# Turning keys and queries in 64-row tiles, both in one block, each row half into its own PSUM bank

## The chip, the core and the metric

The kernel runs on one core of a Trainium2 chip. Times are device microseconds of one launch; the kernel before took 110.33 us (the median of three runs, 109.01 to 110.8). The engines of the core are named as the profile names them: PE (TensorE; PEld is its loading of weights), DVE (VectorE), ACT (ScalarE), POOL (GpSimd) and SP (SyncE, which here issues the loads and stores). The profile shows one execution.

## What is computed

Two layers follow each other: a linear attention with decay, in blocks of 64 positions, and a highway layer over the 512 features that it gives. The inputs are q, k and v of 4 batches x 8 heads x 768 positions x 64, and two 512 x 512 weight matrices.

```
for b in range(nb):                       # 12 blocks of 64 positions
    qb, kb, vb = q[:, :, sl], k[:, :, sl], v[:, :, sl]
    intra = einsum('bhic,bhjc->bhij', qb, kb) * Dmask
    intra = einsum('bhij,bhjd->bhid', intra, vb)
    inter = einsum('bhid,bhde->bhie', qb * lam_pow, kv_state)
    out[:, :, sl] = intra + inter
    kv_state = lam_block * kv_state + einsum('bhsd,bhse->bhde', kb * rev_pow, vb)
x = out.transpose(0, 2, 1, 3).reshape(3072, 512)
H = maximum(x @ w_h, 0);  T = sigmoid(x @ w_t + b_t)
result = T * H + (1 - T) * x
```

## The kernel before

The kernel works in 12 steps of 256 positions (three to a batch), each in two blocks of 128. What runs, in which order, is written out in a string, PLAN: each word is a token, such as `TQ.2.2=5` or `EK.2.2@DVE`. The part before the first dot is the operation, the first number is the step, `@` names the engine that does it, and `=` lists the PSUM banks that it takes, of seven that go around (0 to 6; the eighth holds the running state kv). A table DO gives the function for each token. Every engine executes its own tokens in the order of the plan; waits between engines are put in from the data, the buffers and the banks. A block that takes a bank waits until the last reader of the bank's former content is done. The tokens that matter here, for a step n:

- Lk, Lq, Lv: loads on SP's queue (L192, L195). CK, CQ, CV: the casts to bf16, with the decay for q and v, into kb, qb and vs (from the third step on mostly on POOL, L104, L217, L212).
- TK, TQ: eight full 128 x 128 transposes of keys (L236) or queries (L231) on PE into one bank each. EK, EQ: one copy of 1024 columns out of that bank, into kT or qT (on ACT at L102 or on DVE at L104).
- SS.n.e: scores of n (L253), paired with updates of the state (L258), in 64 x 64 tiles. It needs all of kT and qT. M: the causal mask on DVE (L292), four to a step. KE: a copy of the state (ss).
- I: the part of the output that comes from the state (L308, needs qT and ss). A: the part within a block (L318, needs M). D: copies of the result to xT (L102, L104).
- F.n.u.w: eight matmuls of the highway layer (L336; w is 0 for H, bank bh, and 1 for T, bank bt), u one half of the features. H: relu and difference on DVE (L341). G: two sigmoids on ACT (L350), in place in the bank. X: the product on DVE (L354), which reads that bank last.
- R: turning back, 32 matmuls of 64-row tiles, the row halves alternating between two banks (L383). E: copies of these to o (L102, L104). ST: the store.
- Z: matmuls on zeros at the start (L402).

SS, A, U and S work in 64 x 64 tiles of the array, R of a whole step in 64 x 128 tiles, all others on the full array. kT and qT have two buffers each, kb three and qb two.

Of the kernel before, what the change touches and what calls it, by code (L numbers as in the profile page):

```python
# [14 lines left out]


PLAN = """
Lk.0.0 Lv.0.1 Lv.0.0 Lq.0.0 Lk.0.1 Lq.0.1 Lv.1.1 CK.0.0@POOL Lq.1.0 Z.12=0 TK.0.0=0 Lq.1.1 CV.0.0@DVE Lk.1.0
CQ.0.0@POOL EK.0.0@DVE Lv.1.0 CV.0.1@DVE CK.0.1@ACT Lk.1.1 Z.11=1 TQ.0.0=1 B=2 EQ.0.0@ACT CQ.0.1@POOL W.0.1 W.0.0
Z.6=0 TQ.0.1=3 TK.0.1=4 EQ.0.1@DVE U.0.0 EK.0.1@ACT W.1.1 S.0.0=56 KE.0.0@DVE S.0.1=01 CQ.1.2@POOL W.1.0 M.0.0.1 Z.1=3  # L20
U.0.1 I.0=34 M.0.1.1 KE.0.1@ACT Lk.2.1 M.0.0.0 A.0.1 M.0.1.0 TQ.1.2=0 Lq.2.1 CV.1.2@DVE CK.1.2@ACT EQ.1.2@ACT Lq.2.0
Z.8=1 TK.1.2=1 A.0.0 EK.1.2@DVE Lk.2.0 D.0.0@DVE Z.3=5 SS.1.1=56 WC.0.0.1@ACT WC.0.0.0@POOL M.1.1.0 KE.1.0@ACT
WC.0.1.0@POOL D.0.1@ACT Lv.2.1 WC.0.1.1@DVE Z.4=0 SS.1.0=01 M.1.1.1 I.1=35 KE.1.1@ACT Lv.2.0 F.0.0.0=4 WC.1.1.0@DVE PT
M.1.0.1 Lk.3.1 F.0.1.0=6 M.1.0.0 WC.1.0.0@POOL WC.1.0.1@ACT Lk.3.0 WC.1.1.1@DVE A.1.1 A.1.0 BC F.0.0.1=1 H.0.1 Lq.3.1
D.1.1@ACT H.0.0 D.1.0@ACT F.0.1.1=0 Lq.3.0 CQ.2.2@POOL F.1.0.0=2 Lv.3.0 G.0.1@ACT CK.2.2@DVE F.1.0.1=6 Lv.3.1
G.0.0@ACT X.0.1@DVE TQ.2.2=5 Lq.4.0 X.0.0@DVE TK.2.2=4 EQ.2.2@ACT CV.2.2@POOL F.1.1.0=3 Lq.4.1 EK.2.2@DVE G.1.0@ACT
H.1.0 SS.2.0=01 Lk.4.1 H.1.1 CK.3.2@POOL SS.2.1=54 Lk.4.0 M.2.0.1 F.1.1.1=2 KE.2.0@ACT M.2.1.0 Lv.4.0 TK.3.2=3 M.2.1.1
CQ.3.2@POOL G.1.1@ACT I.2=15 M.2.0.0 Lv.4.1 A.2.1 X.1.0@DVE A.2.0 Lk.5.0 R.0=40 D.2.0@ACT D.2.1@DVE CV.3.2@POOL
TQ.3.2=6 E.0.0@ACT Lk.5.1 F.2.1.1=1 E.0.1@ACT EQ.3.2@DVE Lq.5.1 EK.3.2@ACT X.1.1@DVE F.2.1.0=5 CQ.4.2@POOL Lq.5.0
R.1=40 H.2.1 SS.3.1=62 Lv.5.0 F.2.0.0=3 CK.4.2@POOL KE.3.0@ACT M.3.1.1 Lv.5.1 E.1.1@ACT M.3.1.0 SS.3.0=52 E.1.0@ACT  # L30
H.2.0 Lq.6.0 TQ.4.2=0 KE.3.1@ACT CV.4.2@POOL M.3.0.1 TK.4.2=6 G.2.1@ACT Lq.6.1 F.2.0.1=4 M.3.0.0 EQ.4.2@ACT EK.4.2@DVE
Lv.6.0 I.3=32 A.3.0 CK.5.2@POOL A.3.1 Lk.6.1 SS.4.1=56 D.3.0@ACT D.3.1@DVE TK.5.2=0 KE.4.0@ACT M.4.1.1 Lk.6.0
F.3.0.0=2 G.2.0@ACT CQ.5.2@POOL EK.5.2@DVE Lv.6.1 SS.4.0=36 H.3.0 F.3.0.1=0 Lq.8.0 M.4.0.0 CV.5.2@POOL M.4.0.1
TQ.5.2=2 Lk.9.0 G.3.0@ACT F.3.1.0=3 X.2.1@DVE Lq.7.0 EQ.5.2@ACT X.2.0@DVE F.3.1.1=6 CQ.6.2@POOL M.4.1.0 Lq.7.1
KE.4.1@ACT I.4=14 H.3.1 G.3.1@ACT R.2=25 Lk.8.1 X.3.0@DVE A.4.0 E.2.1@ACT X.3.1@DVE A.4.1 Lk.7.1 SS.5.0=30 E.2.0@ACT
D.4.0@DVE CK.6.2@POOL SS.5.1=56 D.4.1@ACT Lk.7.0 TQ.6.2=2 M.5.0.0 KE.5.0@ACT CV.6.2@POOL TK.6.2=1 M.5.1.1 Lv.7.0
EQ.6.2@ACT F.4.1.0=4 M.5.0.1 Lv.7.1 EK.6.2@ACT F.4.0.0=3 H.4.1 Lk.8.0 M.5.1.0 I.5=62 SS.6.1=01 H.4.0 Lq.8.1 A.5.0
KE.6.0@ACT M.6.1.0 CQ.7.2@POOL R.3=45 Lv.9.1 A.5.1 M.6.1.1 SS.6.0=30 D.5.0@ACT Lv.8.0 F.4.0.1=1 M.6.0.0 D.5.1@ACT
M.6.0.1 Lk.9.1 TQ.7.2=6 G.4.0@ACT CK.7.2@POOL F.5.0.0=3 Lq.10.1 EQ.7.2@ACT F.4.1.1=2 H.5.0 Lk.10.1 E.3.1@ACT X.4.0@DVE
TK.7.2=0 CV.7.2@POOL G.4.1@ACT I.6=63 ST.0 KE.6.1@DVE F.5.0.1=5 X.4.1@DVE Lv.8.1 F.5.1.0=1 G.5.0@ACT CK.8.2@POOL  # L40
EK.7.2@DVE Lq.9.0 A.6.0 E.3.0@ACT H.5.1 A.6.1 SS.7.1=20 Lq.9.1 D.6.0@ACT D.6.1@DVE TK.8.2=4 M.7.1.1 F.6.1.0=1 Lv.9.0
EK.8.2@ACT X.5.0@DVE CK.9.2@POOL F.6.1.1=6 KE.7.0@DVE Lk.10.0 CQ.8.2@POOL H.6.1 R.4=30 SS.7.0=54 Lk.11.1 E.4.0@ACT
F.5.1.1=1 E.4.1@ACT M.7.0.1 G.6.1@ACT ST.4 M.7.1.0 TK.9.2=3 Lq.10.0 M.7.0.0 TQ.8.2=0 G.5.1@ACT CV.8.2@POOL F.6.0.0=4
EQ.8.2@DVE Lk.11.0 KE.7.1@ACT X.5.1@DVE I.7=25 EK.9.2@ACT Lq.11.0 A.7.0 H.6.0 A.7.1 CQ.9.2@POOL SS.8.0=01 X.6.1@DVE
D.7.1@ACT Lv.10.1 SS.8.1=34 M.8.0.1 D.7.0@ACT F.6.0.1=6 KE.8.0@DVE Lq.11.1 CK.10.2@POOL F.7.0.0=5 M.8.1.0 G.6.0@ACT
M.8.1.1 ST.3 TQ.9.2=1 CV.9.2@POOL H.7.0 F.7.1.0=2 EQ.9.2@ACT Lv.10.0 X.6.0@DVE TK.10.2=3 M.8.0.0 ST.1 I.8=45
EK.10.2@ACT CQ.10.2@POOL H.7.1 SS.9.1=61 A.8.1 KE.9.0@ACT M.9.1.0 A.8.0 R.5=02 M.9.1.1 SS.9.0=36 CK.11.2@POOL
E.5.1@DVE F.7.0.1=1 KE.9.1@ACT M.9.0.1 E.5.0@ACT F.7.1.1=2 D.8.0@DVE D.8.1@ACT ST.5 CQ.11.2@POOL M.9.0.0 G.7.0@ACT
Lv.11.1 TK.11.2=6 Lv.11.0 I.9=04 F.8.1.0=5 EK.11.2@ACT ST.2 X.7.0@DVE TQ.10.2=3 G.7.1@ACT H.8.1 CV.10.2@POOL F.8.0.0=1
EQ.10.2@ACT R.6=65 H.8.0 A.9.1 X.7.1@DVE A.9.0 SS.10.1=31 D.9.0@ACT D.9.1@DVE F.8.1.1=2 E.6.1@ACT M.10.1.1 F.9.1.0=0  # L50
E.6.0@DVE G.8.1@ACT M.10.1.0 ST.6 TQ.11.2=4 CV.11.2@POOL KE.10.0@DVE F.9.1.1=5 EQ.11.2@ACT X.8.1@DVE SS.10.0=16
G.9.1@ACT H.9.1 R.7=32 M.10.0.1 KE.10.1@ACT F.8.0.1=4 X.9.1@DVE E.7.0@ACT M.10.0.0 E.7.1@ACT I.10=06 SS.11.0=53
G.8.0@ACT ST.7 A.10.0 M.11.0.0 A.10.1 SS.11.1=21 D.10.1@ACT X.8.0@DVE F.9.0.0=5 KE.11.0@ACT M.11.1.0 D.10.0@ACT
F.9.0.1=6 M.11.0.1 M.11.1.1 F.10.1.0=4 G.9.0@ACT H.9.0 I.11=20 X.9.0@DVE A.11.0 A.11.1 R.8=31 D.11.0@ACT R.9=56
E.8.0@ACT F.10.0.0=2 E.9.0@DVE E.9.1@ACT E.8.1@ACT D.11.1@DVE ST.9 F.10.1.1=3 H.10.0 ST.8 F.10.0.1=6 H.10.1 G.10.1@ACT
F.12.1.1=5 G.10.0@ACT X.10.1@DVE F.11.1.1=1 F.11.1.0=0 G.12.1@ACT X.10.0@DVE F.11.0.1=2 G.11.1@ACT H.11.1 F.12.1.0=4
R.10=36 G.11.0@ACT H.12.1 X.11.1@DVE F.11.0.0=0 E.10.0@ACT X.12.1@DVE F.12.0.1=4 E.10.1@ACT H.11.0 F.12.0.0=1
G.12.0@ACT X.11.0@DVE ST.10 R.11.1.1=5 H.12.0 R.11.0.2=3 E.11.1.1@DVE X.12.0@DVE E.11.0.2@ACT ST.11.1.1 R.11.1.0=0
ST.11.0.2 E.11.1.0@DVE ST.11.1.0
"""  # L60

BUFS = dict(kf=5, qf=5, vf=5, kb=3, qb=2, vs=3, kT=2, qT=2, m=8, xT4=2, th4=2, xT2=3, xT1=2, th2=2, th1=2, hm2=3, hm1=2, tb2=2, tb1=2, ss=4, o=5, oh=2, oq=1)
# [3 lines left out]
def kernel(  # L66
# [13 lines left out]
    C = 128  # L80
# [4 lines left out]
    J = 2  # L85
# [11 lines left out]
    def half(e):  # L97
        return slice(64 * e, 64 * e + 64)
# [80 lines left out]
    def get(*key):  # L179
        return made[key]  # L180
# [57 lines left out]
    def evac_k(n, p, eng):  # L238
        hs = heads(p)
        copy(eng, new(("kT", n), [128, NP, J, C])[:, hs.start // 2:hs.stop // 2], get("ktr", n, p))  # L240

    def evac_q(n, p, eng):
        hs = heads(p)
        if n:
            copy(eng, new(("qT", n), [128, NP, 2 * C]).rearrange("e h (p j) -> e h p j", j=Q),
                 get("qtr", n, p).rearrange("e j (p h) -> e h p j", h=NP))
            return
        copy(eng, new(("qT", n), [128, NP, 2 * C])[:, hs.start // 2:hs.stop // 2].rearrange("p n (c j) -> p n c j", j=J),
             get("qtr", n, p).rearrange("p n j c -> p n c j"))


    def score(n, e, hp, j, b):
        T.matmul(get("s", n, e, hp // 2)[half(b), hp % 2, j, :], lhsT=get("kT", n)[half(e), hp, j, half(b)],  # L253
                 rhs=get("qT", n)[half(e), hp, b * C:(b + 1) * C], start=True, stop=True)
# [6 lines left out]
    def scores_state(n, e, bk):  # L261
        for u in range(2):
            bank(("s", n, e, u), bk[u], [128, 2, J, C])
        b = 1 - e
        st = [(hp, j, x) for hp in range(NP) for j in range(J) for x in range(2)]
        if b == 1 and n % NST == NST - 1:
            st = []
        for i, (hp, j, x) in enumerate((hp, j, x) for hp in range(NP) for j in range(J) for x in range(2)):
            score(n, e, hp, j, x)
            if st:  # L270
                state(n, b, *st[i])

    def scores(n, u, bk):
        for e in range(2):
            bank(("s", n, e, u), bk[e], [128, 2, J, C])
        for hp in (2 * u, 2 * u + 1):
            for j in range(J):
                for e in range(2):
                    for b in range(2):
                        score(n, e, hp, j, b)  # L280

    def states(n, b):
        for hp in range(NP):
            for j in range(J):
                for e in range(2):
                    state(n, b, hp, j, e)
# [111 lines left out]
    def spin(r, bk, idle=[0]):  # L398
# [8 lines left out]
        "CK": lambda a, e, bk: cast_k(*a, e), "CQ": lambda a, e, bk: cast_q(*a, e), "CV": lambda a, e, bk: cast_v(*a, e),  # L407
        "TK": lambda a, e, bk: trans("k", *a, bk), "TQ": lambda a, e, bk: trans("q", *a, bk),
        "EK": lambda a, e, bk: evac_k(*a, e), "EQ": lambda a, e, bk: evac_q(*a, e),
        "SS": lambda a, e, bk: scores_state(*a, bk), "S": lambda a, e, bk: scores(*a, bk), "U": lambda a, e, bk: states(*a),  # L410
        "KE": lambda a, e, bk: evac_s(*a, e), "M": lambda a, e, bk: mask(*a),
        "I": lambda a, e, bk: inter(*a, bk), "A": lambda a, e, bk: intra(*a), "D": lambda a, e, bk: take(*a, e),
# [42 lines left out]
```

## Time and profile before

| | |
|---|---|
| median of three runs | 110.33 us (109.01 to 110.8) |
| the profiled execution | 109.92 us |
| its span in the profile | 108.2 us |
| granted TensorE clock | 1.0 of full speed |
| key transposes, L236 | 96 of 219 ns each from start to modelled end, 7.5 us busy |
| query transposes, L231 | 88 of 220 ns each, 6.8 us busy |
| DMA | 27.59 MB, 255 GB/s on average |

The busy time of a group counts overlapping instructions once; the matmuls of a block overlap, so 96 transposes of 219 ns each take 7.5 us together and not 21. A group's row gives the line, the engine, the operation, what it writes and reads, the count, busy us and mean ns of one, and the idle time of the engine ahead of it with what ended it. The chain of waits gives the start, the length and the work of each piece that the end hung on. A timeline row gives start, length, engine, line and operation, and in brackets the idle time ahead and what ended it.

### The profile page before, as it was taken

The page shows a single profiled execution, that of the slowest core. Times are in us where ns is not written, and L with a number is a line of the kernel's source. Part 1 is how long each engine was busy: PE and PEld are TensorE (multiplying, and loading weights), DVE is VectorE, ACT ScalarE, POOL GpSimd, SP SyncE. Part 2 cuts the span into 40 slices and gives each one's busy share as a digit, 9 for nine tenths or more (in the row PEclk, how much of TensorE's full clock was granted, in tenths as well). Part 3 has the DMA queues.
Part 4 walks back from the last instruction along what each step waited for, and adds up shares of the span by engine and source line. Part 5 has one row for each costly group of instructions (what it writes and reads, how often), then busy time and mean ns, then how long its engine had stood idle before and what let it go on. Part 6 is the DMA issues. An engine that isn't in the chain of part 4 may idle for free.

```text
span 108.2 us, 4978 instructions
## 1 busy us (share of the span) xinstructions
PE 100.8 (93%) x2190; PEld 81.1 (75%) x2190; DVE 84.5 (78%) x144; ACT 70.7 (65%) x131; POOL 55.5 (51%) x48
## 2 busy tenths in 40 slices
PE   4999999999999999998999999999999899999950
PEld 1334564588897888887889888979898688899940
DVE  4027595878798897999795996999977988958870
ACT  0534263696875499498668757957697788676940
POOL 7027530437999889992973975974760600000000
PEclk9999999999999999999999999999999999999999
DMA  1799999999999999999999991789969443107264
GB/s 30 201 267 321 313 365 382 353 306 286 298 336 294 321 321 309 300 311 309 253 316 327 366 312 51 265 226 329 346 197 286 149 165 139 61 6 295 98 227 161
DMA packets 34397, 27.59 MB, mean 255 GB/s; under 512 B 1732, under 2 KB 27592, under 8 KB 34376
## 3 DMA queue, kind: packets, MB, share of 16 engines
q1 hardware_dynamic: 34080, 27.27, 82.5%
q8 instruction: 17, 0.28, 1.1%
q10 hardware_dynamic: 296, 0.01, 0.1%
q14 instruction: 4, 0.03, 0.1%
HBM read 20.98 MB, written 6.29 MB: 252 GB/s over the span
## 4 chain that ended last, share of the span: by engine, by line
PE 71%; DVE 11%; DMA 5%; issue 4%; ACT 4%; SPq 1%; POOL 1%; POOLq 0%; DVEq 0%
PE bt L336 17%; PE bh L336 16%; PE bs L253 8%; PE bx L383 5%; DMA qf<-in_q_dram 5%; DVE m L292 5%; PE bo L318 5%; PE bspin L402 5%; PE bktr L236 4%; PE bqtr L231 4%; PE bo L308 3%; DVE th L354 3%; DVE hm L341 2%; PE kv L258 2%; SPq L195 1%
## 5 line engine op out<-in xcount | busy, mean ns | idle before, releaser
L336 PEld LDWEIGHTS <-w_b 128*128 128x128 bf16 x416 | 36.4, 98 | 5.3 <-issue 0.8
L292 DVE TENSOR_TENSOR m<-bs,tri 128x512 bf16<-128x512 f32 x48 | 31.1, 682 | 3.0 <-PE bs L253 2.7
L350 ACT ACTIVATE bt<-bt,bt_col 128x256 f32<-128x256 f32 (+1 forms) x52 | 22.0, 432 | 7.9 <-PE bt L336 4.4
L217 POOL TENSOR_TENSOR qb<-qf,pow_q 128x1024 bf16<-128x1024 f32 x11 | 20.9, 1903 | 9.5 <-DMA qf<-in_q_dram 7.1
L336 PE MATMUL bt<-xT,w_b 128*128 128x256 bf16 (+1 forms) x208 | 24.5, 265 | 0.7 <-issue 0.5
L336 PE MATMUL bh<-xT,w_b 128*128 128x256 bf16 (+1 forms) x208 | 25.0, 265 | 0.0
L212 POOL TENSOR_TENSOR vs<-vf,pow_v 128x1024 bf16<-128x1024 f32 x10 | 19.0, 1902 | 7.3 <-PE bt L336 4.7
L341 DVE SCALAR_TENSOR_TENSOR hm<-bh,xT 128x512 bf16<-128x512 f32 (+1 forms) x26 | 16.5, 643 | 3.7 <-PE bh L336 2.4
L354 DVE TENSOR_TENSOR th<-bt,hm 128x512 bf16<-128x512 f32 (+1 forms) x26 | 16.5, 643 | 2.2 <-ACT bt L350 2.1
L402 PE MATMUL bspin<-blank,id 128*128 128x512 bf16 x45 | 13.4, 447 | 1.4 <-POOL id masks.py:199 1.4
L253 PE MATMUL bs<-qT,kT 64*64 64x128 bf16 x384 | 14.0, 218 | 0.7 <-DVE th L354 0.4
L102 ACT ACTIVATE ss<-kv 128x512 bf16<-128x512 f32 x15 | 8.9, 596 | 6.7 <-PE bs L253 5.5
L253 PEld LDWEIGHTS <-kT 64*64 64x64 bf16 x384 | 11.0, 106 | 3.1 <-issue 1.5
L104 POOL CAST kb<-kf 128x1024 bf16<-128x1024 f32 (+1 forms) x10 | 9.9, 995 | 4.7 <-DMA kf<-in_k_dram 4.7
L102 ACT ACTIVATE xT<-bo 128x512 bf16<-128x512 f32 x16 | 9.2, 597 | 4.4 <-PE bo L318 4.4
L102 ACT ACTIVATE o<-bx 128x512 f32<-128x512 f32 x19 | 10.5, 596 | 1.5 <-PE bx L383 1.5
L102 ACT ACTIVATE qT<-bqtr 128x1024 bf16<-128x1024 bf16 (+1 forms) x10 | 9.8, 976 | 1.5 <-PE bqtr L231 1.1
L402 PEld LDWEIGHTS <-id 128*128 128x128 bf16 x45 | 4.5, 109 | 7.1 <-issue 2.8
L318 PE MATMUL bo<-m,vs 64*64 64x128 bf16 x384 | 9.1, 219 | 0.4 <-DVE m L292 0.4
L258 PE MATMUL kv<-vs,kb 64*64 64x64 bf16 x320 | 9.4, 196 | 0.0
L102 ACT ACTIVATE kT<-bktr 128x1024 bf16<-128x1024 bf16 (+1 forms) x7 | 6.7, 962 | 2.1 <-PE bktr L236 2.1
L318 PEld LDWEIGHTS <-vs 64*64 64x64 bf16 x384 | 6.5, 106 | 2.1 <-issue 1.2
(61 smaller groups left out, 115.8 us busy)
## 6 DMA issues: line engine op xcount, KB each, us to landing
kf<-in_k_dram SPq DMA_DIRECT2D x24, 256.0 KB, 6.3
vf<-in_v_dram SPq DMA_DIRECT2D x24, 256.0 KB, 5.7
qf<-in_q_dram SPq DMA_DIRECT2D x24, 256.0 KB, 5.6
out_dram<-o SPq DMA_DIRECT2D x11, 512.0 KB, 3.4
w_f<-in_moe_w_h_dram SPq DMA_DIRECT2D x2, 512.0 KB, 7.6
w_f<-in_moe_w_t_dram SPq DMA_DIRECT2D x2, 512.0 KB, 8.7
out_dram<-oh SPq DMA_DIRECT2D x2, 128.0 KB, 1.9
out_dram<-oq SPq DMA_DIRECT2D x1, 256.0 KB, 2.2
```

Source lines behind the costliest of these rows:

```text
L102: A.activation(dst, src, AF.Copy)
L212: ENG[eng].tensor_tensor(dst, in0=get(src, n)[:, heads(p)].rearrange("p h (j d) -> p h j d", j=J), in1=pw[:, n % NST, heads(p), :, None].t ...
L217: ENG[eng].tensor_tensor(new(("qb", n), [128, Q, 2, D]).rearrange("p j e d -> p e j d"), in0=get("qf", n).rearrange("p e (j d) -> p e j d" ...
L253: T.matmul(get("s", n, e, hp // 2)[half(b), hp % 2, j, :], lhsT=get("kT", n)[half(e), hp, j, half(b)], rhs=get("qT", n)[half(e), hp, b * C ...
L258: T.matmul(kv[half(e), hp, half(e)], lhsT=get("kb", n)[half(b), j, 2 * hp + e, :], rhs=get("vs", n)[half(b), 2 * hp + e, j, :], start=firs ...
L292: V.tensor_tensor(new(("m", n, e, u), [128, 2, J, C]), in0=get("s", n, e, u), in1=tri[:, None].to_broadcast([128, 2, J, C]), op=ALU.mult)
L318: T.matmul(get("o", n, b)[half(e), hp, :], lhsT=get("vs", n)[half(b), 2 * hp + e, j, :], rhs=get("m", n, e, u)[half(b), hp % 2, j, :], sta ...
L336: T.matmul(t[:, r, :], lhsT=w_b[w][:, kc, (2 * u + r) * 128:(2 * u + r + 1) * 128], rhs=get("xT", *g)[:, kc, :], start=(kc == 0), stop=(kc ...
L341: V.scalar_tensor_tensor(new(("hm", g, u), [128, 2, z * C], tag=f"hm{z}"), in0=get("h", g, u), scalar=0.0, in1=get("xT", *g)[:, 2 * u:2 * ...
L350: A.activation(dst[:, r, :], src[:, r, :], AF.Sigmoid, bias=bt_col[:, 2 * u + r:2 * u + r + 1])
L354: ENG[eng].tensor_tensor(new(("th", g), [128, NP, z * C], tag=f"th{z}")[:, 2 * u:2 * u + 2, :], in0=get("tt", g, u), in1=get("hm", g, u), ...
L402: T.matmul(t, lhsT=id128, rhs=blank, start=True, stop=True)
```

## The change

From the third step on (n = 2 to 11), TK and TQ become one token, T. It makes 32 transposes instead of 16: for keys, then queries, for each of eight column groups, one for each half of the 128 rows. Row half r goes into the r-th bank of the token, keys and queries side by side in that bank. EK and EQ become two copies each, FK.n.r and FQ.n.r, one for each bank, of 512 columns; they are on the engine that had the whole copy. T stands in the plan where the later of TK and TQ stood, and the copies behind it, so the copy of the earlier one has moved back. The order of all other tokens is the same, and so are the buffers; the bank numbers of the whole plan are dealt anew. Two further tokens, VK and VQ, are defined and not used.

```diff
-G.0.0@ACT X.0.1@DVE TQ.2.2=5 Lq.4.0 X.0.0@DVE TK.2.2=4 EQ.2.2@ACT CV.2.2@POOL F.1.1.0=3 Lq.4.1 EK.2.2@DVE G.1.0@ACT
+G.0.0@ACT X.0.1@DVE Lq.4.0 X.0.0@DVE T.2=31 FQ.2.0@ACT FQ.2.1@ACT CV.2.2@POOL F.1.1.0=6 Lq.4.1 FK.2.0@DVE FK.2.1@DVE
+G.1.0@ACT H.1.0 SS.2.0=02 Lk.4.1 H.1.1 CK.3.2@POOL SS.2.1=31 Lk.4.0 M.2.0.1 F.1.1.1=4 KE.2.0@ACT M.2.1.0 Lv.4.0
...
+M.4.0.1 T.5=04 FK.5.0@DVE FK.5.1@DVE Lk.9.0 G.3.0@ACT F.3.1.0=5 X.2.1@DVE Lq.7.0 FQ.5.0@ACT FQ.5.1@ACT X.2.0@DVE
...
+F.4.1.1=5 H.5.0 Lk.10.1 E.3.1@ACT X.4.0@DVE T.7=13 FQ.7.0@ACT FQ.7.1@ACT CV.7.2@POOL G.4.1@ACT I.6=62 ST.0 KE.6.1@DVE
+F.5.0.1=0 X.4.1@DVE Lv.8.1 F.5.1.0=5 G.5.0@ACT CK.8.2@POOL FK.7.0@DVE FK.7.1@DVE Lq.9.0 A.6.0 E.3.0@ACT H.5.1 A.6.1
...
+X.7.0@DVE T.10=34 FK.10.0@ACT FK.10.1@ACT G.7.1@ACT H.8.1 CV.10.2@POOL F.8.0.0=1 FQ.10.0@ACT FQ.10.1@ACT R.6=03 H.8.0
...
+    def turned(x, n, i):
+        if x == "k":
+            return get("kb", n)[:, i % J, 2 * (i // J):2 * (i // J) + 2, :]
+        return get("qb", n)[:, i]
+
+    def trans_rows(n, bk):
+        for r in range(2):
+            bank(("tr", n, r), bk[r], [128, 2, 8, 64], BF16)
+        for i, x in enumerate("kq"):
+            for c in range(8):
+                for r in range(2):
+                    T.transpose(get("tr", n, r)[:, i, c, :], turned(x, n, c)[half(r)], id128[half(r), half(r)])
...
+    def rows(x, n, r):
+        return get("tr", n, r)[:, "kq".index(x)] if ("tr", n, r) in made else get(x + "v", n, r)
+
+    def evac_k_rows(n, r, eng):
+        copy(eng, new(("kT", n), [128, NP, J, C])[:, :, :, half(r)].rearrange("e h j p -> e (h j) p"), rows("k", n, r))
+
+    def evac_q_rows(n, r, eng):
+        copy(eng, new(("qT", n), [128, NP, 2 * C])[:, :, r * C:(r + 1) * C].rearrange("e h (p j) -> e h p j", j=Q),
+             rows("q", n, r).rearrange("e j (p h) -> e h p j", h=NP))
```

## The prediction

> **What bounds the kernel now.** I read the page's busy shares first, then the groups of instructions with shapes kept apart, the chain of waits in order of time, the busy time by stretches, and last the timelines of single engines around each transpose. Every engine works through its tokens in the order of the plan, so each row of a timeline can be given its token.
>
> ```profile
> PE 100.8 (93%) x2190; PEld 81.1 (75%) x2190; DVE 84.5 (78%) x144; ACT 70.7 (65%) x131; POOL 55.5 (51%) x48
> ```
>
> ```profile
> 66.00:80.00 14.00, 13.76 (x336) 12.40 (x329) 13.26 (x22) 10.82 (x21) 11.21 (x7) 1.00 0.75 243
> 80.00:92.00 12.00, 11.53 (x318) 9.91 (x317) 10.23 (x17) 9.56 (x18) 2.12 (x2) 1.00 0.59 196
> 92.00:104.00 12.00, 12.00 (x258) 10.91 (x255) 9.70 (x20) 9.01 (x22) 0.00 (x0) 1.00 0.29 107
> ```
>
> The columns of the second view are the stretch, its length, then the busy time of PE, PEld, DVE, ACT and POOL, the granted clock (1.00 throughout), the DMA share and GB/s. TensorE has no idle time to speak of from 28 to 104 us, but VectorE is nearly as full (13.26 of 14 us from 66 to 80), and TensorE runs only a few tenths of a us ahead of the copies that free its seven rotating banks. So time taken from TensorE counts only where the next block finds its bank free and its operand copied. POOL's casts are not the limit: kb and qb of a step are written 1.8 us (step 2) to over 7 us (step 11) before its last transpose block.
>
> **The prices.**
>
> ```profile
> L236 PE MATMUL bktr<-id,kb 128*128 128x128 bf16 x96 | 7.5, 219 | 0.1
> L383 PE MATMUL bx<-id,xT 64*128 64x64 bf16 x176 | 6.8, 191 | 0.0
> L231 PE MATMUL bqtr<-id,qb 128*128 128x128 bf16 x88 | 6.8, 220 | 0.0
> ```
>
> ```profile
> 79.32 0.45 PE bktr L236 x8
> ...
> 88.16 0.57 PE bx L383 x32
> ...
> 95.23 1.04 PE bx L383 x64
> 96.27 0.98 PE bh L336 x8
> 97.25 2.64 PE bt L336 x32
> ```
>
> Removed per step from step 2 on: two blocks of 8 full transposes, 0.45 us each, 0.89 together. Added: 32 transposes of 64 rows, which the trace of before doesn't have, but L383's have their very shape (64*128, 64 columns, alternating halves, two banks): 32 more of those cost 1.04 - 0.57 = 0.47 us. The block after them takes 0.98 instead of the usual 0.87, and one ahead of them is stretched alike: about 0.1 us each time the array changes its tile size. T costs 0.66 us between full-size blocks, 0.57 behind SS or R. The gain is 0.23 to 0.4 us a step, some 2.7 us of TensorE over ten steps. The bounds of the unshown rate: 14.7 ns an instruction (L383's pairs) and 28 ns (half of a full transpose's 56, no pairing); I take the first, the nearer row.
>
> The Trainium skill, TensorE: Matmul & The Clock Gate, section Back-to-back issue gap, gives a matmul of 1 to 64 columns a floor of about 25 ns. By that floor 32 of them would take 0.80 us, and nearly all of the gain were gone; L383's 14.7 ns says that it does not hold across two row halves.
>
> ```profile
> L102 ACT ACTIVATE qT<-bqtr 128x1024 bf16<-128x1024 bf16 x9 | 9.2, 1018 | 1.1 <-PE bqtr L231 1.1
> L102 ACT ACTIVATE qT<-bqtr 128x512 bf16<-128x512 bf16 x1 | 0.6, 597 | 0.4 <-PE bqtr L236 0.4
> ...
> L104 DVE COPY kT<-bktr 128x1024 bf16<-128x1024 bf16 x5 | 3.4, 684 | 1.2 <-PE bktr L236 1.1
> ...
> L104 DVE COPY qT<-bqtr 128x1024 bf16<-128x1024 bf16 x2 | 2.4, 1224 | 0.4 <-PE bqtr L231 0.4
> ...
> L104 DVE COPY qT<-bqtr 128x512 bf16<-128x512 bf16 x1 | 0.7, 691 | 1.7 <-PE bqtr L236 1.7
> ...
> L104 DVE COPY kT<-bktr 128x512 bf16<-128x512 bf16 x1 | 0.4, 410 | 0.0
> ```
>
> Copies: 20 of 1024 columns become 40 of 512. Back to back on ACT one follows the last after 0.50 us (two 0.60 copies take 1.08), so a pair takes 1.09 instead of 1.02: fourteen times, 1.0 us of an engine with room. On DVE keys take 0.74 instead of 0.68, queries 1.30 instead of 1.22. The half key copy writes runs of 64; bounds 0.41 (the row above) and 0.69 (the strided row); I take 0.41, since its source is still one run. Work itself is cheap; **what the change costs is order.** (a) Both turns of a step now stand where the later one stood, so copies that ran early now queue up together. (b) The built program makes the second engine's copy of a bank wait for the first engine's, because keys and queries now share each bank: in steps 2 and 4 FK on DVE waits for FQ on ACT, in 5 FQ for FK, in 3 and 8 likewise. Before, they lay in different banks and overlapped. (c) Both banks stay taken until all four copies are done, and all banks are dealt anew.
>
> The Trainium skill, PSUM — Partial Sum Buffer, section PSUM bank collisions raise a hardware error, says that ScalarE and VectorE must not read one bank's same partitions at once. It asks for just these waits; the trace of before has no such pair.
>
> **The walk.** I followed both plans with these durations and 0.04 us from an engine's end to the start it releases; a copy can start 0.23 us after T's last issue (L383's 0.19 and 0.04). "Lag" is start after minus start before.
>
> Step 2: T.2 ends its issue at 28.48. FQ on ACT 28.70 to 29.80, then FK.2.1 on DVE to 30.26 (one key copy to 29.71 before). SS.2.0 starts at 30.30 instead of 29.79. DVE has no idle time from 29 to 34, so H, M and A.2.0 follow: lag 0.55, which step 3 keeps.
>
> Step 4: T.4 gains 0.33, but G.2.1 and the two FQ keep ACT until 42.50 and FK.4.1 ends at 42.96: SS.4.1 at 43.00 instead of 41.91, lag 1.1. TK.5's absence then gives 0.4 back.
>
> Step 5: FK.5 no longer runs early; behind T.5 it holds X.2.1 on DVE until 48.22, and X.2.1 now frees the bank of F.3.1.1 (X.2.1 wasn't in its way before). F.3.1.1 starts at 48.27 instead of 46.74, lag 1.5. Step 6: F.4.1.0 at 52.43, lag 0.95. TQ.7's absence brings 0.45.
>
> Step 7, the clearest place:
>
> ```profile
> 57.05 0.93 ACT L350 ACTIVATE bt<-bt,bt_col 128x256 f32<-128x256 f32 x2 [0.39 <-ACT xT L102]
> 57.90 1.02 ACT L102 ACTIVATE qT<-bqtr 128x1024 bf16<-128x1024 bf16 x1
> 58.80 0.60 ACT L102 ACTIVATE o<-bx 128x512 f32<-128x512 f32 x1
> 59.28 0.94 ACT L350 ACTIVATE bt<-bt,bt_col 128x256 f32<-128x256 f32 x2
> ```
>
> These are G.4.0, EQ.7, E.3.1 and G.4.1. The query copy was done before G.4.1; now both FQ.7 wait for T.7 and stand ahead of it. From T.7's first issue: 0.68 to FQ.7.0, 1.0 for the two, 0.93 for G.4.1, 0.76 for X.4.1 and its two releases: 3.4 us, and then F.5.1.0 gets its bank, which X.4.1 now frees. TensorE has only T.7, I.6 and F.5.0.1 for that time, 0.57 + 0.22 + 0.87 = 1.66: it stands for 1.7 us. Lag 2.4. TK.8's absence gives nothing, F.6.1.0 waits for xT (D.6.1).
>
> Step 8: G.5.1 stands behind FK.8 on ACT, X.5.1 behind it on DVE; the full DVE of 66 to 80 us passes it on. Lag 2.7 at F.6.0.1. Step 9: TK.10's absence gives 0.45 and T.9 takes 0.2 more than TQ.9, but four copies now follow each other on ACT: 0.68 + 1.5 + 0.6 + 0.05 = 2.83 from T.9 to SS.9.1, against a cover of 0.57 + 0.87 + 0.54 = 1.99. Lag 2.7 - 0.25 + 0.85 = 3.3. Step 10: TK.11's absence and T.10 again make -0.25; R.6 takes a bank of T.10, read last by FQ.10.0, which stands behind two FK and G.7.1: 0.68 + 1.0 + 0.83 + 0.6 + 0.05 = 3.16, cover T.10 and F.8.0.0 = 1.54. Lag 3.3 - 0.25 + 1.6 = 4.7. Step 11: the 0.6 us that TensorE idled after TQ.11, with no releaser in the profile, I take not to recur, T.11 adds 0.2, and R.7 waits likewise for FQ.11.1, 0.7 more: lag 5.0. Then TensorE is busy throughout (12.00 of 12 us from 92 to 104), the copies catch up, and nothing gives the lag back.
>
> The profiled execution took 109.92 us, 1.7 more than its span of 108.2: 109.92 + 5.0 = **114.9 us**, that is 4.1% over the median of 110.33 (the execution lay 0.4% under that). 2% is about what a measurement here can tell from no change.
>
> **Rivals.** (1) As forecast, 0.62. (2) TensorE's gain arrives and the waits vanish in the slack of ACT (65%): 109.9 - 2.7 = 107.2; for it speaks 93% on PE, against it the few tenths of slack per bank; 0.07. (3) Only the two longest stands remain, steps 7 and 10, 1.7 + 1.6 - 2.7 = +0.6: 110.5; for it, that a lag gives DVE and ACT time to catch up; 0.18. (4) The halves do not pair: 0.43 more in T, which heads the waiting chain in eight steps, +3.4: 118.3; slower still, 0.09; the skill's 25 ns floor, named above, points this way. (5) The half key copies on DVE run at 0.69: 0.56 more in steps 2, 4 and 5, 116.6; 0.04. The case on the other side, (2), decides if F.5.1.0, R.6 and SS.4.1 start within 0.2 us of the block ahead.
>
> The range reaches from 110.5, the middle of (3), to 118.3, which takes in (4) and (5); it leaves out (2) and the lower half of (3), 0.16. Chances: faster by over 2% (under 108.1) 0.06, nearly all of (2); within 2% 0.22, which is (3) and the edges of (1) and (2); slower 0.72.
>
> **What would show it.** In the profile after: 64*128 transposes with 15 ns between issues; PE busy some 3 us less, with idle time of about 7 us in the middle, released by ACT copies qT and kT and by DVE th L354; key copies on DVE starting after the query copies end in steps 2 and 4. I am wrong if TensorE stays above 92% busy, or if the copies of one bank overlap.

## The result, and the profile after

The changed kernel takes **119.58 us** (median of four runs, 118.51 to 120.24) against 110.49 for the kernel before on the same chip: 1.089 times as long, with a 95% interval of 1.071 to 1.108. Medians here and below are of all runs, ratios and intervals of those in the chip's faster state alone, so the two can differ (119.58 over 110.49 is 1.082). The forecast was 114.9 in a range up to 118.3. The direction was right, the size was not: the time lies 4.7 us over the forecast and 1.3 over the range. The profiled execution took 118.51 us, with a span of 116.8 against 108.2 before, so 8.6 us more.

First the busy shares on the page of the changed kernel:

```profile
PE 99.8 (85%) x2348; PEld 77.5 (66%) x2350; DVE 86.4 (74%) x150; ACT 71.6 (61%) x145; POOL 56.0 (48%) x48
```

TensorE went from 93% to 85%. Its busy time fell by only 1.0 us, and its idle time grew by 9.6 (17.0 us against 7.4). Where it lies shows in the busy time by stretches of the changed kernel (stretch, length, busy time and count of PE, PEld, DVE, ACT and POOL, granted clock, DMA share, GB/s):

```profile
28.00:42.00 14.00, 12.65 (x370) 10.16 (x365) 11.83 (x20) 9.68 (x20) 13.15 (x10) 1.00 1.05 308
42.00:56.00 14.00, 10.55 (x312) 8.36 (x302) 10.76 (x19) 8.50 (x19) 9.24 (x6) 1.00 0.99 278
56.00:66.00 10.00, 8.48 (x216) 7.19 (x214) 7.10 (x12) 7.17 (x16) 6.83 (x6) 1.00 1.05 320
66.00:80.00 14.00, 13.14 (x343) 10.66 (x343) 12.46 (x22) 7.84 (x17) 8.82 (x6) 1.00 0.62 190
80.00:92.00 12.00, 10.10 (x311) 8.54 (x309) 9.01 (x15) 8.32 (x17) 4.13 (x3) 1.00 0.63 206
92.00:104.00 12.00, 11.58 (x340) 9.98 (x337) 9.73 (x16) 9.45 (x21) 1.58 (x1) 1.00 0.25 92
```

From 28 to 104 us TensorE stands idle for 9.5 us, where it stood for 1.2 before. (A *stand*, here and below, is a stretch in which TensorE issues nothing; its length is counted from one issue to the next.) The clock is full throughout, so nothing of this is a slower clock. What ended the idle time is in the waits of PE (who waited, for whom, us in total, times, longest):

```profile
PE bx L415 <- ACT qT L103: 1.7, 2, 1.4
PE bh L368 <- DVE th L386: 1.5, 1, 1.5
...
PE btr L264 <- issue: 1.4, 1, 1.4
PE kv L290 <- issue: 1.4, 2, 1.1
...
PE bs L285 <- ACT qT L103: 0.8, 4, 0.3
```

The first two and the last are the stands that the prediction walked to: R.6 behind the query copies, F.5.1.0 behind X.4.1, and the score blocks behind the copies. The two rows with "issue" are something else: TensorE waited, and nothing that the profile shows released it. The second place of those, in a timeline of PE:

```profile
54.87 0.40 PE L264 MATMUL btr<-id,qb 64*128 64x64 bf16 x15 [1.42 <-issue]
```

This is the middle of T.6. Half of its transposes have gone out, qb has long been written and both banks are held, and yet the next transpose comes 1.60 us after the last (1.42 of it idle, since the modelled end of a transpose covers 0.2). There are three such stands, 0.47 us in SS.3.1 at 38.20, 1.31 in SS.4.1 at 44.39 and this one: 3.4 us. The kernel before has three as well, 0.57, 0.20 and 0.69, together 1.5. For the first of these the profile does name a releaser:

```profile
47.67 0.68 DVE L341 SCALAR_TENSOR_TENSOR hm<-bh,xT 128x512 bf16<-128x512 f32 x1
48.26 1.28 DVE L354 TENSOR_TENSOR th<-bt,hm 128x512 bf16<-128x512 f32 x2
49.72 0.64 PE L253 MATMUL bs<-qT,kT 64*64 64x128 bf16 x22 [0.36 <-DVE th L354]
```

But the last row is SS.5.0, whose banks 3 and 0 were last read by H.3.1 (done at 48.35) and X.3.0 (the first of the two at 48.26, done at 48.9). The product that ended at 49.54, X.3.1, reads bank 6, which SS.5.0 does not take. So the engine named was not what it waited for.

What they have in common shows when TensorE's instructions are numbered in the order of issue (a matmul and its weight load are two) and set beside the packets of the DMA queue that the page calls "instruction":

```profile
q8 instruction: 18, 0.29, 1.1%
```

The kernel before had 17 such packets. Each is 16,384 bytes long. Before has 4,389 numbered instructions, after 4,706; one packet for 256 instructions makes 17.1 and 18.4. These stands all end at the same number modulo 256. (Idle times of 0.2 us with "issue" stand at other numbers too, in both kernels, and are left out.)

```
kernel  stand ends at  length  place    number mod 256  packet lands  stand ends after it
before       49.72      0.57   SS.5.0        193            48.26            1.46
before       65.30      0.20   R.4           193            63.85            1.44
before       86.54      0.69   F.9.1.1       193            85.22            1.32
after        38.20      0.47   SS.3.1        191            36.53            1.67
after        44.39      1.31   SS.4.1        191            43.08            1.31
after        54.87      1.60   T.6           191            53.54            1.32
```

(Two records seem to be missing early in the trace of after, hence 191 for 193; why it is 193 and not 0 the traces do not show.) So TensorE stands at the edge of a block of 256 instructions until about 1.3 to 1.7 us after the next 16 KB of its own program have landed. This reading is an inference from one trace each; the experiments test it.

The prices of the change itself, from the groups of the changed kernel with shapes kept apart:

```profile
L103 ACT ACTIVATE qT<-btr 128x512 bf16<-128x512 bf16 x16 | 8.7, 599 | 3.1 <-PE btr L264 3.0
...
L264 PE MATMUL btr<-id,kb 64*128 64x64 bf16 x160 | 4.2, 191 | 0.1
L264 PE MATMUL btr<-id,qb 64*128 64x64 bf16 x160 | 4.2, 190 | 1.4 <-issue 1.4
...
L105 DVE COPY kT<-btr 128x512 bf16<-128x512 bf16 x8 | 3.2, 421 | 1.2 <-ACT qT L103 0.9 <-PE btr L264 0.2
...
L105 DVE COPY qT<-btr 128x512 bf16<-128x512 bf16 x4 | 2.6, 686 | 0.6 <-PE btr L264 0.3 <-ACT kT L103 0.3
```

A T without a stand issues its 32 transposes in 0.45 us, 14.5 ns each. The half copies take 599 ns on ACT, and 421 (keys) and 686 (queries) on DVE. The key copies on DVE wait for "ACT qT", the query copies on DVE for "ACT kT": the copies of one bank follow each other.

### The profile page after: what moved, and what is told of

Same layout as the page of the kernel before. It is cut to its first block, busy times and chain, and to the rows that moved or that the text cites. A ratio compares the mean times of both kernels' runs of the same rounds, so it can differ in the third digit from the quotient of the medians.

```text
span 116.8 us, 5314 instructions
## 1 busy us (share of the span) xinstructions
PE 99.8 (85%) x2348; PEld 77.5 (66%) x2350; DVE 86.4 (74%) x150; ACT 71.6 (61%) x145; POOL 56.0 (48%) x48
## 4 chain that ended last, share of the span: by engine, by line
PE 56%; ACT 14%; DVE 12%; issue 6%; DMA 5%; POOL 1%; SPq 1%; POOLq 0%; DVEq 0%
PE bt L368 15%; PE bh L368 13%; PE bs L285 5%; PE bx L415 5%; DMA qf<-in_q_dram 5%; ACT qT L103 5%; PE btr L264 5%; PE bspin L434 4%; PE bo L350 4%; DVE m L324 4%; ACT kT L103 3%; DVE th L386 3%; DVE hm L373 3%; ACT bt L382 3%; PE bo L340 2%
## 5 line engine op out<-in xcount | busy, mean ns | idle before, releaser
L285 PE MATMUL bs<-qT,kT 64*64 64x128 bf16 x384 | 15.6, 219 | 1.7 <-ACT qT L103 0.8
L434 PE MATMUL bspin<-blank,id 128*128 128x512 bf16 x43 | 12.5, 432 | 1.5 <-POOL id masks.py:199 1.4
L290 PE MATMUL kv<-vs,kb 64*64 64x64 bf16 x320 | 10.0, 196 | 1.4 <-issue 1.4
L103 ACT ACTIVATE qT<-btr 128x512 bf16<-128x512 bf16 x16 | 8.7, 599 | 3.1 <-PE btr L264 3.0
L290 PEld LDWEIGHTS <-kb 64*64 64x64 bf16 x320 | 7.6, 107 | 3.2 <-issue 2.8
L415 PE MATMUL bx<-id,xT 64*128 64x64 bf16 x176 | 7.0, 191 | 1.8 <-ACT qT L103 1.7
```

Of the source, the lines that this page charges most:

```text
L103: A.activation(dst, src, AF.Copy)
L290: T.matmul(kv[half(e), hp, half(e)], lhsT=get("kb", n)[half(b), j, 2 * hp + e, :], rhs=get("vs", n)[half(b), 2 * hp + e, j, :], start=firs ...
L434: T.matmul(t, lhsT=id128, rhs=blank, start=True, stop=True)
```

## The experiments

At this point there were three readings, with the letters that the expectations use. **A**: the order of the work (both turns late, the copies in a row, banks dealt anew) makes nearly the whole loss. **B**: the loss is the sharing of banks between the copies of two engines. **C**: the order makes some 2 to 4 us, and the 320 instructions that TensorE gets in addition (160 matmuls with their weight loads) make the rest, since blocks of its program come too late. A rival **D** to C is that the stands are waits for data that the profile does not name, and so belong to their places in the program and not to the block's edge. Runs 1 to 4 share one median of before, 109.74 us, runs 5 to 8 share 109.6, runs 9 and 10 share 109.39.

### 1. The order alone

The changed plan and banks, with the full-size transposes and whole copies of before; keys and queries have a bank each:

```diff
-T.7=13 FQ.7.0@ACT FQ.7.1@ACT CV.7.2@POOL G.4.1@ACT
+TK.7.2=1 TQ.7.2=3 EQ.7.2@ACT CV.7.2@POOL G.4.1@ACT      (and so in every step from 2 to 11)
```

> The changed plan with its bank numbers and its later place for both turns, but with full 128-row transposes, each operand into a bank of its own, and whole copies of 1024 columns at the places of the first half copies. So the order is that of the change, and the paired transposes, the shared banks and the 320 further TensorE instructions are gone. Theory A (most of the loss is the order in which copies queue and banks come free): the long stands of TensorE at F.5.1.0 and R.6 stay, 1.5 us or more each, and the time is 115 to 117 us. Rival B (the loss is the sharing of banks between two engines' copies): those stands shrink under 0.5 us and the time is 110 to 112.5. Rival C (the loss is the loading of TensorE's code, which stalls where 256 instructions run in under some 5 us): idle time without a releaser as before, about 1.2 us in all, and 112 to 114 us.

Measured: 113.24 us, ratio 1.034 [1.028, 1.040]. That is 3.7 us, in C's bounds, too little for A and too much for B. (These 3.7 us, and the 4.7 of run 2, go by the ratio.) In its waits the stand at F.5.1.0 is the largest behind the start:

```profile
PE bh L367 <- DVE th L385: 1.6, 1, 1.6
PE bspin L433 <- POOL id masks.py:199: 1.4, 1, 1.4
PE bs L284 <- ACT qT L102: 0.9, 3, 0.4
PE bh L367 <- DVE xT L104: 0.7, 2, 0.4
```

It lasts 1.84 us from issue to issue, against 1.79 in the changed kernel. The stand at R.6 is not there: R.6 takes over a bank that now holds only keys, and their copy is done before G.7.1. After 21 us no stand without a releaser is longer than 0.2 us, where C had expected some 1.2 us in all, as before.

### 2. The instructions alone

The kernel before, with 320 more TensorE instructions and no other change: twenty highway blocks make their products in 128 columns and not 256.

```diff
+        cs = [slice(0, 128), slice(128, 256)] if i in (2, 4, 6, 8, 10) else [slice(0, z * C)]
-            for kc in range(KC):
-                T.matmul(t[:, r, :], lhsT=..., rhs=get("xT", *g)[:, kc, :], ...)
+            for c in cs:
+                for kc in range(KC):
+                    T.matmul(t[:, r, c], lhsT=..., rhs=get("xT", *g)[:, kc, c], ...)
```

> The kernel before with 320 further TensorE instructions and nothing else: the matmuls of 20 blocks of the highway layer (groups 2, 4, 6, 8 and 10) are split into halves of 128 columns, 160 more pairs of weight load and matmul for the same columns, in the same banks and the same order. The splitting itself costs 2 x 56 - 109 = 3 ns a pair, 0.5 us. Theory C (code loading): TensorE stands more often at every 256th instruction, 1.5 to 3 us more in all, 112.5 to 114 us. Theory A alone: only the 0.5 us, 110.5 to 111.5 us.

Measured: 115.08 us, ratio 1.043 [1.029, 1.056]. Plan, banks, transposes and copies are those of before, and it costs 4.7 us, more than C had asked for; the interval reaches from 3.2 to 6.1. The profiled execution was the shortest of the four, 113.44 us. The waits of PE in this run:

```profile
PE bs L253 <- issue: 1.9, 2, 1.6
PE bspin L404 <- POOL id masks.py:199: 1.4, 1, 1.4
PE bh L338 <- issue: 1.2, 1, 1.2
```

The stands end at 39.90 (1.43), 44.17 (0.52), 55.15 (0.59), 59.42 (1.85) and 94.17 us (0.23), 4.6 us together, and every one at number 193 modulo 256. The split products themselves add only 0.5 us to the busy time of their groups (50.0 against 49.5 us), as was reckoned.

### 3. The same copies, dealt by bank

In steps 2, 3, 4, 5 and 8 ACT copies the first bank of T (keys and queries) and DVE the second, so that neither waits for the other:

```diff
-FQ.4.0@ACT FQ.4.1@ACT FK.4.0@DVE FK.4.1@DVE
+FQ.4.0@ACT FQ.4.1@DVE FK.4.0@ACT FK.4.1@DVE
```

> The changed kernel with one difference: in steps 2, 3, 4, 5 and 8, where keys and queries are copied by two engines, the copies are dealt by bank and not by operand (first bank on ACT, second on DVE), at the same places of the plan. No copy waits for the other engine's any more. If the waits on a shared bank cost what the prediction says (0.5 us at SS.2.0, 0.7 at SS.4.1, some tenths in 5 and 8, part of it taken back later): 117 to 118.5 us, and SS.2.0 starts within 0.2 us of the block ahead. If they cost nothing: 119 to 120 us.

Measured: 117.45 us, ratio 1.070 [1.060, 1.079]. Beside run 4 below, on the same chip and as long as the changed kernel (1.093 [1.085, 1.101]), that is 2.2 us less. The waits between copies of a bank are real and cost something. SS.2.0 was expected to follow the block ahead within 0.2 us and still stands 0.46, behind a key copy on ACT (0.43 and 0.49 in two parts in run 4). The stands at block edges are 4.1 us in its trace, where the changed kernel has 3.4: five of them, all at 193 modulo 256. That fits a TensorE that waits less for copies and so reaches the edge of its block earlier.

### 4. The edges moved by 120 instructions

The changed kernel, with four zero matmuls fewer and 64 tiny ones more at its very start, long before anything waits. Every edge then falls 120 instructions earlier in the work:

```diff
-Z.12=0
+Z.8=0
+        for _ in range(64 if idle[0] == 1 else 0):
+            T.matmul(t[:, 0:4], lhsT=id128, rhs=blank[:, 0:4], start=True, stop=True)
```

> The changed kernel with 60 more pairs of TensorE instructions at the very start (four large matmuls on zeros fewer, 64 of 4 columns more), so that every 256th instruction falls 120 instructions earlier in the work. Theory C: the two long stands without a releaser (in SS.4.1 and T.6 of the changed kernel, 1.3 and 1.6 us) leave those places; such stands still begin at instruction 191 to 193 of each 256, about 1.3 us after a code load ends, and their sum may be larger or smaller by 2 us: 117 to 121 us. Rival D (they are waits for data that the profile doesn't name): they stay in SS.4.1 and T.6 with their lengths, 119 to 120 us.

Measured: 119.61 us, ratio 1.093 [1.085, 1.101]. The time is that of the changed kernel, and the stands have moved. SS.4.1 and T.6 have none. They are now in T.4 (ends at 41.00, 1.39), at 46.37 (0.49), in T.7 (61.67, 1.39) and in a score block (83.97, 1.56), all at 193 modulo 256, 4.8 us together. That is 1.4 more than in the changed kernel, while its profiled execution took only 0.7 more (119.18 against 118.51), so the stands do not simply add up:

```profile
PE btr L264 <- issue: 2.4, 2, 1.2
PE bx L415 <- ACT qT L103: 1.7, 2, 1.4
PE bh L368 <- DVE th L386: 1.5, 1, 1.5
PE bspin L434 <- POOL id masks.py:199: 1.4, 1, 1.4
PE bs L285 <- issue: 1.3, 1, 1.3
```

The stands that follow from the order, R.6 behind "ACT qT" and F.5.1.0 behind "DVE th", stayed where they were. D is out.

### 5 and 6. Half of the loads left out

The profile counts the packets of the program on the same 16 DMA engines as the inputs, whose share is near 1 up to 66 us. Both kernels were run with the loads of the odd steps from 3 on left out; the casts of an odd step read the tiles of the step before it, so those steps are computed from other inputs:

```diff
+    def held(n):
+        return n - 1 if n % 2 and n > 2 else n
     def load(x, n, p, eng):
+        if held(n) != n:
+            return
```

> The changed kernel with half of its loading left out: from step 3 on the loads of k, q and v of the odd steps are not issued, and the casts of an odd step read the tiles of the step before it (so the output of these steps is another). All work on the engines is the same. Theory C (TensorE's next 256 instructions are loaded through the same DMA engines and come late behind the input loads): the stands at every 256th instruction, 3.4 us in all in the changed kernel, fall under 1 us, and the time is 115 to 117 us. If the loads have no part in them: 119 to 120 us.

> The kernel before with the same loads left out, as the reference for the run with the changed kernel. Theory C: it loses only its own 1.3 us of such stands, 108 to 109.5 us, so the change costs 6 to 8 us here instead of 9 to 10. If the loads have no part: about 109.7 us, and the change costs 9 to 10 us still.

Measured: the changed kernel 116.88 us (1.069 [1.062, 1.076]), the kernel before 108.75 (0.996 [0.991, 1.000]). The distance is 8.1 us, just past the upper end of what C gave (6 to 8). For the kernel before the interval does not exclude that nothing changed. The stands at block edges fell from 1.5 to 0.4 us in the kernel before, and from 3.4 to 2.6 in the changed one, not below 1. The profiled execution of the changed kernel took 1.1 us less than without this edit (117.44 against 118.51), of which the stands are 0.8. So the load of the DMA engines is a part of it and not all: the changed kernel still stands 1.59 us at 39.31 and 1.03 at 45.23.

### 7. Two words of the plan moved

The order stands of steps 7 and 10 were aimed at alone: G.4.1 ahead of FQ.7, and FQ.10 ahead of G.7.1.

```diff
-T.7=13 FQ.7.0@ACT FQ.7.1@ACT CV.7.2@POOL G.4.1@ACT
+T.7=13 G.4.1@ACT FQ.7.0@ACT FQ.7.1@ACT CV.7.2@POOL
-G.7.1@ACT H.8.1 CV.10.2@POOL F.8.0.0=1 FQ.10.0@ACT FQ.10.1@ACT R.6=03
+FQ.10.0@ACT FQ.10.1@ACT G.7.1@ACT H.8.1 CV.10.2@POOL F.8.0.0=1 R.6=03
```

> The changed kernel with two moves in ACT's order and nothing else: in step 7 the sigmoid G.4.1 stands ahead of the two query copies, in step 10 the two query copies stand ahead of the sigmoid G.7.1. Theory A: F.5.1.0 finds its bank free (stand 1.8 us, now under 0.5) and R.6 waits about 0.8 us less; the time falls by 1.5 to 2.5 us against the changed kernel, to 117 to 118.3 us. If these stands are not on the path or are replaced by others: 119 to 120 us.

Measured: 117.19 us, ratio 1.067 [1.057, 1.077]. The stand ahead of F.5.1.0 went from 1.79 to 0.26 us, that in R.6 from 1.60 to 0.75. These are 2.4 us, and the median fell by 2.4. The profiled executions differ by 2.8 (115.72 against 118.51), and there it is not these two stands alone: those at block edges are 2.6 us here against 3.4, and a new stand of 0.47 us behind DVE th has come in at 88.54.

### 8. All that removes order stands

Copies by bank in steps 2, 3, 4, 5, 8, 9, 10 and 11, G.4.1 ahead of FQ.7, X.2.1 ahead of FK.5.

> The changed kernel with all waits that theory A names loosened: copies dealt by bank (first bank on ACT, second on DVE) in steps 2, 3, 4, 5, 8, 9, 10 and 11, G.4.1 ahead of the query copies of step 7, and X.2.1 ahead of the key copies of step 5. Theory A with C: what the order costs is mostly back (3 to 4 us) and what the code loads cost stays: 114.5 to 117 us, still over the kernel before. If the order were all of the loss: 110 to 111.5 us.

Measured: 116.96 us, ratio 1.067 [1.059, 1.075], no better than run 7, though its order stands are smaller. The waits of PE say why:

```profile
PE kv L290 <- issue: 2.0, 2, 1.2
PE bspin L434 <- POOL id masks.py:199: 1.4, 1, 1.4
PE btr L264 <- issue: 1.1, 1, 1.1
PE bo L350 <- DVE m L324: 1.0, 3, 0.5
PE bo L350 <- issue: 1.0, 1, 1.0
```

The rows "DVE th" and "ACT qT" of 1.4 us and more are gone; those with "issue" make 4.1, and from issue to issue the stands at block edges make 5.0 us (1.01, 1.44, 1.33 and 1.24), against 2.6 in run 7. What the order gave back, the late blocks took.

### 9. One word moved where no block is late

Run 1 has no stand at a block edge, so in it a stand that goes should be worth its length:

```diff
-TK.7.2=1 TQ.7.2=3 EQ.7.2@ACT CV.7.2@POOL G.4.1@ACT
+TK.7.2=1 TQ.7.2=3 G.4.1@ACT EQ.7.2@ACT CV.7.2@POOL
```

> The kernel of e1 (order, banks and full-size transposes) with one word moved: G.4.1 ahead of EQ.7, so that F.5.1.0 does not wait for the query copy. No TensorE instruction is added and e1 had no stand at a code block behind its first 20 us. If the price of the changed order is paid by order stands alone, and a stand that goes is given back wherever no code block is late, then nearly the whole 1.6 to 1.8 us of the stand ahead of F.5.1.0 comes back: 111.4 to 111.9 us. If the copies and VectorE pass a lag on whatever stands ahead (the gain is eaten further on), less than half comes back: 112.4 to 113.2.

Measured: 111.92 us, ratio 1.023 [1.016, 1.029], 1.3 us under run 1 (1.2 by the ratios, whose intervals just touch; the two ran on different chips). The stand is gone. In the timeline of PE F.5.0.1 and F.5.1.0 follow each other:

```profile
60.21 1.04 PE L367 MATMUL bt<-xT,w_b 128*128 128x256 bf16 x8
61.08 1.04 PE L367 MATMUL bh<-xT,w_b 128*128 128x256 bf16 x8
```

In run 1 they stand 2.60 us apart:

```profile
59.72 1.04 PE L367 MATMUL bt<-xT,w_b 128*128 128x256 bf16 x8
62.32 1.03 PE L367 MATMUL bh<-xT,w_b 128*128 128x256 bf16 x8 [1.57 <-DVE th L385]
```

Of the 1.8 us of the stand some 1.3 arrive; the time lies at the very edge of the 111.4 to 111.9 us that were expected if a stand that goes is given back. Two small stands at block edges came in, 0.36 us at 44.39 and 0.20 at 54.87, both at number 191.

### 10. Run 8 with half of the loads

The edits of runs 8 and 5 together.

> The kernel of e8 (copies by bank, G.4.1 ahead of FQ.7, X.2.1 ahead of FK.5) with the loads of the odd steps from 3 on left out; their casts read the tiles of the step before, so half of the positions are computed from other inputs. Theory C (the order stands and the late code blocks are the two causes): e8's stands at code blocks, 5.4 us, fall by 1 to 3 us with the emptier DMA queues, and nothing else stands: 113.5 to 116.0 us. If something else than the queues' load makes the blocks late (TensorE runs through a block faster than the next one can be fetched in any case), the stands stay within 0.7 us of 5.4, and the time is 116.2 to 117.2.

Measured: 114.03 us, ratio 1.043 [1.035, 1.051], 2.9 under run 8 (2.6 by the ratios). The stands at block edges fell from 5.0 to 2.7 us, which is 2.3 of it. Two are left and did not shrink, 1.24 at 38.51 and 1.44 at 44.43:

```profile
PE kv L295 <- issue: 2.2, 2, 1.2
```

No run with T in it came under 1.04 of the kernel before, and of those with the changed order run 9 came nearest, at 1.023. What makes those two blocks late with half of the loads gone was not found.

## Why the prediction was wrong

**The walk held in the main.** The places where it said that TensorE would stand do stand, and from step 5 on close to the length given. F.5.1.0 in step 7, said to stand 1.7 us, adds 1.68 to the lag; ACT's timeline shows the order that was named, both FQ.7 and then the sigmoids of G.4.1 and G.5.0:

```profile
63.22 1.09 ACT L103 ACTIVATE qT<-btr 128x512 bf16<-128x512 bf16 x2 [0.82 <-PE btr L264]
64.19 1.78 ACT L382 ACTIVATE bt<-bt,bt_col 128x256 f32<-128x256 f32 x4
65.90 0.59 ACT L103 ACTIVATE o<-bx 128x512 f32<-128x512 f32 x1
```

R.6 in step 10 adds 1.58 us (1.6 said), R.7 in step 11 0.66 (0.7 said: 0.18 ahead of it and 0.48 within). F.3.1.1 in step 5 adds 0.64 to the lag of the block ahead of it (0.6 said: 1.1 less 0.4, with 0.2 for T.5, and then 1.5). TK.8's absence gave nothing, TK.10's gave 0.44 and TK.11's 0.45 back. The walk's first term was wrong: of the 0.55 us of lag in step 2 SS.2.0 has 0.07 (29.86 against 29.79), mostly since T.2 began at 27.59 and not where TQ.2 had begun, at 27.93.

**What failed is one step above all, and it was a term that the sum lacked.** The walk priced the added transposes by L383's issue (0.47 us for 32) and by nothing else: 320 more instructions cost TensorE no more than their own issue. And of the kernel before it said that "the 0.6 us that TensorE idled after TQ.11, with no releaser in the profile, I take not to recur". That row was the sign: it is the stand at 86.54 in the table above, at the edge of a block of 256.

```profile
86.55 1.05 PE L336 MATMUL bt<-xT,w_b 128*128 128x256 bf16 x8 [0.47 <-issue]
```

In the changed kernel the edges fall elsewhere, and there TensorE stands three times. The lag of each block, from the two traces, and what the stands at the edges make of it (those of after less those of before up to there):

| block | lag, predicted | lag, measured | of it stands at edges | the rest |
|---|---|---|---|---|
| SS.4.1 (step 4, from its second score on) | 1.1 | 1.08 | 0.47 | 0.61 |
| F.3.1.1 (step 5) | 1.5 | 2.72 | 1.78 | 0.94 |
| F.4.1.0 (step 6) | 0.95 | 3.73 | 2.81 | 0.92 |
| F.5.1.0 (step 7) | 2.4 | 5.37 | 2.81 | 2.56 |
| F.6.0.1 (step 8) | 2.7 | 5.68 | 2.61 | 3.07 |
| A.8.1 (step 9) | 3.3 | 6.22 | 2.61 | 3.61 |
| A.9.1 (behind R.6) | 4.7 | 7.60 | 2.61 | 4.99 |
| F.8.0.1 to the end | 5.0 | 7.85 | 1.92 | 5.93 |

Down to R.6 the last column follows the walk within 0.6 us, and from step 6 on within 0.4. Some of that is luck: the half us too much of step 2 is cancelled between F.3.1.1 and F.4.1.0, where the walk takes 0.55 off and the last column falls by 0.02. At the end the walk stands at 5.6 and not 5.0 if the 0.6 after TQ.11 is counted with the edges, where it belongs: 5.93 against 5.6. That subtraction is arithmetic on two traces, not an experiment, and it treats the stands as if they added up. Run 9 shows that they nearly do where blocks are hardly late (1.3 of 1.8 us arrived, while 0.6 of stands at edges came in), run 8 that they are exchanged where blocks are late. The two runs that take one cause alone say 3.7 us (order, without the shared banks) and 4.7 us (instructions), 8.4 us together, where the whole change costs 9.8 on the 109.74 of their chip. The rest no run assigns; the shared banks are in neither, and by run 3 they cost about 2 us where two engines copy.

**The account of the miss.** 118.51 us of the profiled execution against 114.9 is 3.6 us: 2.6 from the stands at edges (3.4 less the 0.8 at 49.72 and 65.30 of before), 0.3 that the walk was short, and 0.75 behind the last copy to the output's tile, which ends 105.2 us into a span of 108.2 before and 113.1 into 116.8 after; the last stores took that much longer to land, which the walk did not look at (the rounding and the 0.69 taken as 0.6 make up the rest). The median lies another 1.1 over the profiled execution, which was the shortest of four; what the others have more no trace shows.

**The rivals.** (2), the gain arriving, was far off: 107.2. (3) had the two longest stands right and forgot that the others are real too. (4) fell at once: the halves pair, 14.5 ns an instruction, and 118.3 would have been near the time for a wrong reason. The floor of about 25 ns that the Trainium skill gives (TensorE: Matmul & The Clock Gate, section Back-to-back issue gap) does not hold across the two row halves in this trace either. (5) fell with 421 ns for the key half on DVE, where 0.41 was taken.

**The signs named in advance.** The 15 ns between issues, the copies of a bank in a row and TensorE under 92% came as said. Idle time between 28 and 104 us grew by 8.3 us, about 7 were said, but a third of it has no releaser, which was not said. PE's busy time fell by 1.0 and not by about 3: 0.2 us of each stand is shown as busy, since the modelled end of the instruction ahead covers it.

## What to carry to other kernels

When the diff changes the number of instructions on an engine that is nearly full, count them in blocks as well as in nanoseconds: here 320 more instructions alone cost about as much as the change of order alone (ratios 1.043 [1.029, 1.056] and 1.034 [1.028, 1.040]). An idle row with "issue" as its releaser on the busiest engine is to be priced, not passed over; number the instructions and see whether such rows fall on one remainder. And where two limits lie close together, a repair of the one shows up as the other: compare stands by kind before saying that a repair does nothing.

## What the runs showed of the hardware

**TensorE waits for its own program.** In all twelve traces every stand without a releaser that is longer than 0.2 us, after the first 21 us, falls on one number modulo 256, 193 (191 in the changed kernel and in runs 5 to 10, where a few records are missing), and they move when the program ahead of them grows by 120 instructions (run 4). In the traces of before and after, at the edges where TensorE stands, it is 4.0 to 6.2 us from edge to edge with the stand; the packet of 16 KB starts 0.9 to 3.9 us after the edge before and is under way for 1.0 to 1.7 us, and the first instruction of the new block comes 1.3 to 1.7 us after the landing. At all edges after 21 us in the twelve traces, with a stand or without, this last time is 1.2 us or more, but for one of 0.90 (the longest stand of run 2). By this reading TensorE stands when the sum of these is over what it needs for a block: up to 1.85 us at one edge and 5.0 us in one run. The Trainium skill, Runtime: NRT & Kernel Launch, section Instruction fetch mechanics, says that each engine fetches its program in 16 KiB blocks of 256 instructions while it executes the one before, and that crossing such an edge costs little and is mostly hidden. The trace agrees on the block and its size. It does not agree on the cost: hidden at most edges, but not at three of them in the changed kernel, where they make 3.4 us.

**The input loads slow it, but they are not all of it.** With half of them gone the stands fall from 1.5 to 0.4 us (before), 3.4 to 2.6 (after) and 5.0 to 2.7 (run 8). Why packets start as late as 3.9 us after an edge is open.

**A transpose of 64 rows in pairs is as fast as it was hoped to be**: 14.5 ns each, and 0.57 us (0.66 with the stretch of the block ahead) for what took 0.89. TensorE's time for the turns did become shorter; the kernel's did not.
